# Strided heads first: a reordered start, new planner constants and a smaller last store in a fused sparse attention and feed-forward kernel

## Chip, cores and metric

The kernel runs on one core of one Trainium2 chip. The metric is the device time of one launch in microseconds (us), of which a median is taken over runs. TensorE is called PE below, VectorE DVE, ScalarE ACT, GpSimd POOL and SyncE SP, as in the profile.

## What is computed

There are 8 batches, 8 heads, 576 positions and a head dimension of 64. The first four heads see a local band, the last four see every 32nd position. The result of attention, 4608 tokens of 512 values, goes through a feed-forward layer of 2048 hidden values.

```python
mask_local = (rel >= 0) & (rel < 32)                    # heads 0..3, rel = row - column
mask_strided = (rel >= 0) & (column % 32 == row % 32)   # heads 4..7
attn = softmax(where(mask, q @ k.T / 8, -1e9)) @ v
x = attn.transpose(0, 2, 1, 3).reshape(4608, 512)
h = x @ w_in                       # 512 x 2048
g = s * relu(h) ** 2 + b
out = g @ w_out                    # 2048 x 512
```

## The kernel before

**Attention.** A batch has four head pairs, m = 0 and 1 for the band, m = 2 and 3 for the strided heads. `pair_steps` makes the PE steps of one pair. For the early batches these are: transposes of q and k (`trans`), whose results are copied from PSUM into `qD_loc` or `qD_str` (queries, two heads side by side) and `kT_loc` or `kTs`; scores (`score`, L623); for batch 0 a matmul ahead of each score that adds -30000 where the mask forbids (`neg_loc`, `neg_str`, L620), and for later batches a multiplication with a mask on DVE after the exponential; the exponential on ACT (L641); the weighted sums with v (`av`, L684), where `v_loc` and `v_str` carry a column of ones, so that the sums of the weights come out as well; the division on DVE or ACT (L701, L711); transposes of the result (`xtrans`, L731) into `xT`, one buffer for each pair.

Later batches replace PE transposes by transposing DMAs, issued on SP: `k_dma`, `q_dma` (from `QS_DMA`, `KB_DMA`, `QB_DMA`, which are 3, 4 and 5, on) and `x_dma`, or `x_out` and `x_in` through DRAM.

**Feed-forward.** Blocks of 512 tokens. `ff1` (L983) multiplies `xT` with `w_in_sb`; ReLU and square go to ACT or DVE; `ff2` (L1238) or, from block 2 on, `ff2_seven` (L951) multiplies with `w_out_sb`. The last two blocks use `ff1_seven` (L1208). Block 0 is special: its matmuls begin as soon as the first of the four `xT` buffers is there, in the order `FIRST = (0, 1, 2, 3)`. The outputs are evicted by DVE (`store`, L882) and stored by SP (L886).

**Loads.** POOL issues casting DMAs, fp32 in memory to fp16 on chip: for batch 0 `load_qk(0)` (band q and k in two halves each, then strided q and k), one DMA for two heads of band v, strided v (`early_v`); then the four quarters of `w_in`, batch 1, four quarters of `w_out`, and from then on `fetch_qk(b + 2)` and `fetch_v(b + 2)` as buffers come free. The other two heads of band v of batch 0 are staged in fp32 by SP inside the buffer of `w_out` (`stage_v`, L311) and cast by POOL (`cast_v`). `rows_before` copies, for the band, the 32 rows ahead of each block of 96 keys.

A DMA that may only start when something else has landed is held back by a small copy that reads what landed (`gate`, L1323 on POOL and L1362 on SP).

**The order.** Nothing is scheduled at run time: each engine works through its own list in order. `Plan` writes these lists when the program is built. It keeps an estimated time `plan.t` of PE, an estimated time `done` of each result, and a free time of each engine. `flush` posts what is ready by these estimates to ACT, DVE or POOL, or to SP (`D`, `X`, `Y`), in the order of readiness plus an offset for each kind of work (`ORDER`). `LAT` is the time from the end of an issue to the use of its result:

```python
LAT = {"A": 70.0, "V": 70.0, "P": 70.0, "D": 12000.0, "X": 7000.0, "Y": 12000.0}
```

Loads get their estimated landing from `landing(cost)`, a running time of one queue:

```python
ring = max(ring, plan.t + 2000.0) + cost
return ring + (6000.0 if plan.t > 60000.0 else 600.0)
```

The main loop takes an attention step when attention is behind `due()`, which follows the progress of both feed-forward halves, and a feed-forward step otherwise. Where nothing is ready ahead of the 16th `ff1` matmul, `keep_running` puts a matmul on constants, a filler (L1502), which nobody reads.

Of the kernel before, what the change touches and what calls it, by code (L numbers as in the profile page):

```python
# [18 lines left out]
class Plan:  # L19
# [7 lines left out]
    LAT = {"A": 70.0, "V": 70.0, "P": 70.0, "D": 12000.0, "X": 7000.0, "Y": 12000.0}  # L27

    def __init__(self, order):
        self.t = 0.0  # L30
        self.SLACK, self.ahead, self.LATER = order["SLACK"], order["ahead"], order
        self.done = {}
        self.pend = []
        self.free = {"A": 0.0, "V": 0.0, "P": 7000.0, "D": 0.0, "X": 0.0, "Y": 0.0}
        self.banks = {}

# [7 lines left out]

    def flush(self):
        while True:
            best = None
            for p in self.pend:
                r = self.ready_at(p[0])
                if r is None or r > self.t:  # L50
                    continue
                if p[1].keys() <= {"A", "V"} and min(
                        self.free[e] for e in p[1]) > self.t + self.SLACK:
                    continue
                k = p[3][0]
                w = r + self.LATER.get(k[0] if isinstance(k, tuple) and k[2:3] != (0,) else None, 0.0)
                if best is None or w < best[0]:
                    best = (w, r, p)
# [7 lines left out]
            p[2](eng)  # L66
            for k in p[3]:
# [4 lines left out]
                self.done[k] = end + (6000.0 if soon else p[4] or self.LAT[eng])  # L72
# [45 lines left out]
class Step:  # L118
    def __init__(self, fn, ns, needs=(), group=None, keys=(), posts=(), after=None):
# [4 lines left out]
ORDER = {"g": 1500.0, "S": 2500.0, "in": 2500.0, "w_mix": 0.0, "wc": 1000.0, "ev": 1000.0,  # L124
         "c21": 1500.0, "c11": 500.0, "c12": 500.0, "C22": -1500.0, "fv": 0.0, "Vb": -400.0,
         "x": -1500.0, "Ub": 1000.0, "xc": -1500.0, "fe": -400.0, "k": 1500.0, "fu": -1500.0,
         "Va": 500.0, "p": 0.0, "c22": 500.0, "Ua": 2500.0, "e": -1500.0, "q": 0.0, "r": 0.0,
         "u": 0.0, "SLACK": 600.0, "ahead": 0.05}
KINDS = ("g", "S", "in", "w_mix", "wc", "Va", "Ua", "Ub", "Vb", "C22", "xc", "q", "k", "r", "x", "e",
         "p", "u", "ev", "fv", "fu", "fe", "c11", "c22", "c21", "c12")  # L130


def varied(order, rnd):

    order = dict(order)
    for kind in rnd.sample(KINDS, rnd.choice((1, 2, 4))):
        order[kind] = rnd.choice((-1500.0, -800.0, -400.0, 0.0, 500.0, 1000.0, 1500.0, 2500.0))
    if rnd.random() < 0.2:
        order["SLACK"] = rnd.choice((400.0, 600.0, 800.0, 1000.0))
    if rnd.random() < 0.2:  # L140
        order["ahead"] = rnd.choice((0.0, 0.05, 0.1, 0.2))
    return order
# [46 lines left out]
def lay_out(ctx, tc, nc, q, k, v, moe_w_in, moe_w_out, moe_s, moe_b, out, order, q_shape, out_shape,  # L189
# [8 lines left out]
    FIRST = (0, 1, 2, 3)  # L198
# [56 lines left out]
    NV = 2  # L255
# [13 lines left out]
    def x_free(b):  # L269
# [23 lines left out]
    vl_stage = w_out_sb.rearrange("p f m -> p (f m)").bitcast(FP32)[:, 0:NL // 2].rearrange(  # L293
        "p (h t d) -> p h t d", h=2, d=D)

# [13 lines left out]
    def stage_v(heads):  # L309
        for h in heads:  # L310
            nc.sync.dma_start(out=vl_stage[LPAD:128, h], in_=v_band(0, h))  # L311

    nc.sync.dma_start(out=ident, in_=h_ident.ap())
    stage_v(range(2))
    nc.sync.dma_start(out=negs, in_=h_neg.ap())
    nc.vector.memset(ones16, 1.0)
    for i in range(2):
        nc.vector.memset(qD_loc[i], 0.0)
        nc.vector.memset(kT_loc[i][:, 0:LPAD], 0.0)
    nc.vector.memset(vl_stage[0:LPAD], 0.0)  # L320
    for i in range(2):
        nc.vector.memset(qD_str[i], 0.0)
    for i in range(NV):
        nc.vector.memset(v_loc[i][:, :, :, D:D + 1], 1.0)
        nc.vector.memset(v_loc[i][0:LPAD, :, 0, :], 0.0)
        nc.vector.memset(v_str[i][:, :, :, D:D + 1], 1.0)
# [11 lines left out]

    def load_qk(b):
        for mm in range(2) if b == 0 else ():  # L340
            hs = slice(2 * mm, 2 * mm + 2)
            for name, src in (("q", q), ("k", k)):
                if mm == 0:
                    loaded[b, name + "l"] = inp.tile([LQ, NL], FP16, tag=name + "l", name=name + "l")
                nc.gpsimd.dma_start(out=h4(loaded[b, name + "l"])[:, hs],
                                    in_=view_l(src, b)[:, hs])
        for name, src in (("q", q), ("k", k)) if b else ():
# [73 lines left out]
    def cast_v(b, loc, mm, key):  # L421
        nt, np_, dst = (LT, 128, v_loc) if loc else (ST, SQ, v_str)

        def g(eng):
            src = vl_stage if loc else loaded[b, "vs"].rearrange(
                "p (h t d) -> p h t d", h=4, d=D)
            for h in range(2 * mm, 2 * mm + 2):
                copy_on(eng, out=dst[b % NV][0:np_, h, :, 0:D], in_=src[:, h])
        n = nt * D
        plan.post([key], {"P": 1000.0} if loc else {"P": 1160.0} if b == 0 else {"A": 2 * (170 + 0.83 * n), "V": 540.0}, g,  # L430
                  [("cast", b, mm) if loc else ("in", "vs", b, mm)])
        if loc:
            rows_before(b, mm, ("cast", b, mm))

    def rows_before(b, mm, key):
# [3 lines left out]
        src = vl_stage[:, :, :, 0:D] if b == 0 and mm == 0 else vl[:, :, :, 0:D]  # L439

        def g(eng):
            copy_on(eng, out=vl[0:LPAD, hs, 1:LT, 0:D], in_=src[128 - LPAD:128, hs, 0:LT - 1])
        plan.post([key], {"P": 800.0} if b == 0 and mm == 0 else {"P": 800.0, "V": 350.0} if b == 0 else {"A": 700.0, "V": 350.0}, g, [("in", "vl", b, mm)])
# [30 lines left out]
    def pair_steps(b, m):  # L474
# [10 lines left out]
        def trans(name, j, group):  # L485
# [19 lines left out]
            s = Step(f, (57 if id_ == (0, 0) else 40) if alone else 35, needs=[("in", name + sfx, b, mm)],  # L505
# [1090 lines left out]
```

## Time and profile before

| | |
|---|---|
| median of 3 runs | 298.2 us (298.0 to 298.53) |
| profiled execution, its own time | 298.86 us |
| its span, first to last instruction | 297.1 us |
| PE busy | 290.5 us, 2802 matmuls |
| weight loads (PEld) busy | 220.0 us |
| DVE, ACT, POOL busy | 235.3, 194.3, 93.7 us |
| granted PE clock | 0.999 |
| moved by DMA | 38.19 MB, of it 18.23 MB on POOL's queue |

A matmul row counts as busy from its start to a modelled end, and neighbours overlap, so the mean duration of a row is longer than its distance to the next. Where a count matters, distances between starts are used.

### The profile page before, as it was taken

How to read it: one execution, taken by the hardware profiler on the slowest of the kernel's cores; microseconds unless marked ns; L12 is line 12 of the kernel's file. 1: busy time of each engine (PE TensorE's matmuls, PEld its weight loads, DVE VectorE, ACT ScalarE, POOL GpSimd, SP SyncE). 2: the span in 40 equal slices, each digit the busy share in tenths (PEclk: the TensorE clock that was granted, in tenths of full speed). 3: DMA queues.
4: the chain of work that ended last, by engine and by line, in shares of the span. 5: the costliest groups of instructions: out<-in, count | busy, mean ns of one | idle time of the engine just before them, and what ended most of it. 6: DMA issues, size and time to landing. Idle time of an engine off the chain costs nothing.

```text
span 297.1 us, 7092 instructions
## 1 busy us (share of the span) xinstructions
PE 290.5 (98%) x2802; PEld 220.0 (74%) x2802; DVE 235.3 (79%) x501; ACT 194.3 (65%) x336; POOL 93.7 (32%) x140
## 2 busy tenths in 40 slices
PE   8999999999999999999999999999999999999995
PEld 3775656666556568889767776768888989999984
DVE  5857888798966988787877896759898588888963
ACT  3577957898838798647774878469877545675400
POOL 8873624601980296009710394100000000000000
PEclk9999999999999999999999999999999999999999
DMA  8999999997999499989999999999230300110214
GB/s 136 189 206 203 218 180 184 223 171 119 109 195 149 67 132 138 170 173 122 148 136 144 182 170 105 143 140 207 44 97 0 108 29 9 71 38 3 95 48 142
DMA packets 106152, 38.19 MB, mean 129 GB/s; under 512 B 85414, under 2 KB 103974, under 8 KB 106118
## 3 DMA queue, kind: packets, MB, share of 16 engines
q0 software_dynamic: 60848, 18.23, 62.7%
q1 hardware_dynamic: 45270, 19.51, 36.0%
q8 instruction: 22, 0.36, 0.5%
q14 instruction: 12, 0.10, 0.1%
HBM read 36.99 MB, written 10.62 MB: 160 GB/s over the span
## 4 chain that ended last, share of the span: by engine, by line
PE 88%; DMA 6%; ACT 2%; DVE 2%; POOL 1%; issue 1%; ACTq 0%
PE ps_f L983 28%; PE ps_f L951 22%; PE ps_f L1238 8%; DMA v_loc<-in_v_dram 6%; PE ps_s L623 5%; PE ps_f L1208 3%; PE ps_a L684 3%; PE ps_s L1502 2%; PE ps_a L1208 2%; PE ps_s L951 2%; PE ps_t L1208 2%; PE ps_s L1208 2%; PE ps_t L951 1%; PE ps_s L1238 1%; PE ps_t L684 1%; PE ps_t L502 1%
## 5 line engine op out<-in xcount | busy, mean ns | idle before, releaser
L983 PE MATMUL ps_f<-xT,w_in_sb 128*128 128x512 f16 (+4 forms) x568 | 115.5, 331 | 0.3 <-ACT u L1009 0.3
L1009 ACT ACTIVATE u<-ps_f 128x512 f16<-128x512 f32 x104 | 61.0, 594 | 32.5 <-PE ps_f L983 31.8
L983 PEld LDWEIGHTS <-w_in_sb 128*128 128x128 f16 x576 | 57.4, 114 | 23.2 <-issue 0.5
L951 PEld LDWEIGHTS <-gT 128*128 128x128 f16 x608 | 58.4, 98 | 9.2
L951 PE MATMUL ps_f<-w_out_sb,gT 128*128 128x256 f16 x376 | 55.6, 273 | 0.0
L1017 ACT ACTIVATE gT<-u 128x1024 f16<-128x1024 f16 x29 | 30.7, 1057 | 0.8
L1238 PE MATMUL ps_f<-w_out_sb,gT 128*128 128x512 f16 x112 | 30.4, 379 | 0.0
L951 PE MATMUL ps_f<-w_mix,gT 128*128 128x256 f16 x176 | 25.1, 273 | 0.0
L641 ACT ACTIVATE p_str<-ps_s 72x432 f16<-72x432 f32 (+1 forms) x46 | 20.7, 482 | 6.4 <-PE ps_s L623 5.8
L711 DVE TENSOR_TENSOR x_nat<-ps_a,rec 96x384 f16<-96x384 f32 (+2 forms) x46 | 24.1, 523 | 0.6
L641 ACT ACTIVATE p_loc<-ps_s 128x384 f16<-128x384 f32 x46 | 21.4, 494 | 4.8 <-PE ps_s L623 4.3
L1019 DVE TENSOR_TENSOR gT<-u 128x1024 f16<-128x1024 f16 x27 | 18.5, 686 | 5.9 <-ACT u L1009 5.4
L819 DVE TENSOR_TENSOR gT<-gT 128x1024 f16<-128x1024 f16 x34 | 22.4, 678 | 0.6 <-ACT gT L1017 0.4
L382 POOL DMA_DIRECT2D v_loc<-in_v_dram x24 | 17.7, 757 | 8.6 <-DMA w_out_sb<-in_moe_w_out_dram 5.7
L951 PEld LDWEIGHTS <-S 128*128 128x128 f16 x176 | 17.1, 98 | 2.9
L1238 PEld LDWEIGHTS <-gT 128*128 128x128 f16 x128 | 11.4, 98 | 7.8
L387 POOL DMA_DIRECT2D v_str<-in_v_dram x16 | 13.0, 816 | 12.3 <-PE ps_f L983 3.6
L684 PEld LDWEIGHTS <-p_str 72*128 72x128 f16 x256 | 12.8, 98 | 5.1 <-ACT p_str L641 0.4
L1323 POOL COPY gate<-kT 1x1 f16<-1x1 f16 x6 | 1.5, 256 | 45.0 <-DMA kT<-ks 45.0
L951 PE MATMUL ps_f<-w_mix,S 128*128 128x256 f16 x112 | 15.5, 273 | 0.0
L701 DVE RECIPROCAL rec<-ps_a 96x6 f32<-96x6 f32 (+2 forms) x47 | 8.6, 182 | 8.6 <-PE ps_a L684 8.4
L1149 ACT ACTIVATE gT<-u 128x1024 f16<-128x1024 f16 x12 | 12.7, 1058 | 1.7 <-DVE u L1128 1.4
(237 smaller groups left out, 529.7 us busy)
## 6 DMA issues: line engine op xcount, KB each, us to landing
out_dram<-o SPq DMA_DIRECT2D x34, 256.0 KB, 2.9
w_in_sb<-in_moe_w_in_dram POOLq DMA_DIRECT2D x4, 512.0 KB, 9.7
w_out_sb<-in_moe_w_out_dram POOLq DMA_DIRECT2D x4, 512.0 KB, 9.9
qs<-in_q_dram POOLq DMA_DIRECT2D x6, 288.0 KB, 8.4
ks<-in_k_dram POOLq DMA_DIRECT2D x6, 288.0 KB, 9.7
v_loc<-in_v_dram POOLq DMA_DIRECT2D x24, 72.0 KB, 9.6
ql<-in_q_dram POOLq DMA_DIRECT2D x4, 288.0 KB, 9.0
kl<-in_k_dram POOLq DMA_DIRECT2D x16, 72.0 KB, 3.6
```

The lines of the kernel that those rows point to most:

```text
L382: nc.gpsimd.dma_start(out=vl[LPAD:128, h, :, 0:D], in_=v_band(b, h))
L641: nc.scalar.activation(out=st["pw", g][0:nk, 0:2 * n * nq], in_=st["s", g][0:nk, 0:2 * n * nq], func=AF.Exp, scale=scale)
L684: nc.tensor.matmul(out=st["pa", g][:, n % 6, :], lhsT=st["pw", gp_][0:nk, i * nq:i * nq + WIDE], rhs=vt[0:nk, 2 * mm + e, j, :])
L711: nc.vector.tensor_tensor(out=x_at(0, cnt), in0=st["pa", g][0:nq, 0:cnt, 0:D], in1=st["rec", g][0:nq, 0:cnt].to_broadcast([nq, cnt, D]), o ...
L819: {"V": nc.vector, "P": nc.gpsimd}[eng].tensor_tensor(out=at(out), in0=at(x), in1=at(y), op=op)
L951: nc.tensor.matmul(out=gts[name, T, t][:, 0] if halves else gts[name, T][:, t], lhsT=lhs(k, t), rhs=rhs(k), start=fresh and k == 0 and (ha ...
L983: nc.tensor.matmul(out=gts["h", T, ft][:, lo:hi], lhsT=w_in_sb[ft // 4][:, ct].rearrange("p (x l) -> p l x", l=4)[:, ft % 4], rhs=xT[ct][: ...
L1009: nc.scalar.activation(out=u, in_=gts["h", T, ft], func=AF.Relu)
L1017: nc.scalar.activation(out=g, in_=u, func=AF.Square)
L1019: nc.vector.tensor_tensor(out=g, in0=u, in1=u, op=ALU.mult)
L1208: nc.tensor.matmul(out=st[bk][:, 256 * t:256 * t + 256], lhsT=lhs(t, c), rhs=rhs(c), start=fresh and t == c == 0, stop=t == c == 1, skip_g ...
L1238: nc.tensor.matmul(out=gts[id_], lhsT=gts[T][:, ft, ts * 128:(ts + 1) * 128], rhs=w_out_sb[:, ft, cols], start=(ft == 0), stop=(ft == NFT ...
```

## The change

- **Start.** `load_first` replaces `load_qk(0)`: strided q and k of two heads, then of the other two, strided v, band q and k whole, band v of all four heads by one casting DMA on POOL. `stage_v`, its clearing and its casts go. `FIRST` is (2, 3, 0, 1), and batches 0 and 1 take their pairs in this order. `w_in` is issued after the casts of strided v, without its gate. DVE clears `qD_str` and the first v buffers first.
- **Masks of batch 0.** `forbid` is a step of its own, one matmul for each bank of scores, which needs only `negs` and a bank.
- **Planner.** `landing` and `shared` estimate loads: each transposing or storing DMA posted on SP puts off all loads under way by 1 us. `LAT` of `D` and `Y` goes from 12 to 10 us, and 3 us less when no load is under way. `late` gives work of batch 0 offsets by pair. `ORDER` has new values. The fetch of q and k of batch b + 2 waits for `qT` in place of its copy `qD` where q comes by transposing DMA.
- **Last output.** The last product of the last block is computed in two halves of 128 columns, each evicted and stored by itself.

The diff, cut to its core:

```diff
-    LAT = {"A": 70.0, "V": 70.0, "P": 70.0, "D": 12000.0, "X": 7000.0, "Y": 12000.0}
+    LAT = {"A": 70.0, "V": 70.0, "P": 70.0, "D": 10000.0, "X": 7000.0, "Y": 10000.0}
...
+    def landing(self, cost, keys, wait=700.0):
+        self.ring = max(self.ring, self.t + 2000.0) + cost
+        for k in keys:
+            self.done[k] = self.ring + wait
+        self.loads.append(keys)
+
+    def shared(self, cost=1000.0):
+        self.loads = [x for x in self.loads if self.done[x[0]] > self.t + 1000.0]
+        for x in self.loads:
+            for k in x:
+                self.done[k] += cost
+        if self.ring > self.t:
+            self.ring += cost
...
             p[2](eng)
+            if eng in "DXY":
+                self.shared()
...
-                self.done[k] = end + (6000.0 if soon else p[4] or self.LAT[eng])
+                self.done[k] = end + (6000.0 if soon else p[4] or self.LAT[eng] - (
+                    3000.0 if eng in "DY" and self.ring < self.t else 0.0))
...
-    FIRST = (0, 1, 2, 3)
+    FIRST = (2, 3, 0, 1)
...
-    def stage_v(heads):
-        for h in heads:
-            nc.sync.dma_start(out=vl_stage[LPAD:128, h], in_=v_band(0, h))
...
-    nc.vector.memset(vl_stage[0:LPAD], 0.0)
...
+    def load_first():
+        for name in "qk":
+            loaded[0, name + "l"] = inp.tile([LQ, NL], FP16, tag=name + "l", name=name + "l")
+        loaded[0, "qs"] = inp.tile([SR, NS], FP16, tag="qs", name="qs")
+        loaded[0, "ks"] = ks[0]
+        for hs in slice(0, 2), slice(2, 4):
+            for name, src in (("q", q), ("k", k)):
+                nc.gpsimd.dma_start(out=h4(loaded[0, name + "s"])[0:64, hs],
+                                    in_=view_s(src, 0)[0:64, hs])
+                if hs.start == 0:
+                    nc.gpsimd.dma_start(out=h4(loaded[0, name + "s"])[64:SQ],
+                                        in_=view_s(src, 0)[64:SQ])
+        early_v(0)
+        for name, src in (("q", q), ("k", k)):
+            nc.gpsimd.dma_start(out=h4(loaded[0, name + "l"]), in_=view_l(src, 0))
+        load_vl(0)
...
-                    s.posts = [([key], {"V": 1520} if id_ == (0, 1) else {"A": 1280, "V": 1520 if loc else 918}, g,
+                    s.posts = [([key], {"V": 918} if id_ == (0, 2) else {"A": 1280, "V": 1520 if loc else 918}, g,
...
-                    s.posts = [([key], {"V": 757} if id_ == (0, 0) else {"A": 640, "V": 757 if loc else 453},
+                    s.posts = [([key], {"A": 640} if id_ == (0, 2) else {"A": 640, "V": 757 if loc else 453},
...
-                if b < PE_MASK:
-                    nc.tensor.matmul(
-                        out=st["s", g][0:nk, c:c + 2 * nq], lhsT=ident[0:nk, 0:nk],
-                        rhs=neg_loc if loc else neg_str, start=True, stop=False)
...
+        def forbid(i, group):
+            n = min(per_s, nt - i)
+            def f():
+                st["s", i // per_s] = bank(group)
+                nc.tensor.matmul(
+                    out=bank(group)[0:nk, 0:2 * n * nq], lhsT=ident[0:nk, 0:nk],
+                    rhs=(neg_loc if loc else neg_str)[:, None, :].to_broadcast([nk, n, 2 * nq]),
+                    start=True, stop=False, skip_group_check=True)
+            return Step(f, 2 * n * nq / 2.4 + 3, needs=[("negs",)], group=group)
...
+            ends = [(t, k, slice(0, 256)) for t in range(2) for k in range(H)]
+            if last and key == "P3":
+                ends = ends[0:H] + [(1, k, slice(128 * c, 128 * c + 128)) for c in range(2)
+                                    for k in range(H)]
...
-                arrive(both(name + "l", b), landing(4600))
+                plan.landing(2400, both(name + "l", b))
...
-        plan.done["raw", "vl", b] = landing(4600)
+        plan.landing(2700, [("raw", "vl", b)])
...
-            arrive(both("vs", b), landing(5000))
+            plan.landing(3300, both("vs", b), 1200)
...
-    load_qk(0)
-    nc.gpsimd.dma_start(
-        out=v_loc[0].rearrange("p h t d -> p (h t) d")[LPAD:128, 2 * LT:4 * LT, 0:D],
-        in_=v.rearrange("b h (t p) d -> b p (h t) d", p=LQ)[0, :, 2 * LT:4 * LT])
-    early_v(0)
+    load_first()
...
     def weights_in(eng):
-        nc.gpsimd.tensor_copy(out=gate[0:8, 2:3], in_=loaded[0, "qs"][64:SQ, 0:1])
         load_w_in()
...
-    plan.post([("in", "vl", 0, 0)] + both("qs", 0), {"P": 2500.0}, weights_in, [("w",)])
+    plan.post(both("vs", 0), {"P": 2500.0}, weights_in, [("w",)])
...
-        for m in range(4):
+        for m in FIRST if b < 2 else range(4):
...
-                        [("q", (b, mk)) for mk in range(4)] + [("k", (b, mk)) for mk in range(4)] +
+                        [("qT" if b >= (QB_DMA if mk < 2 else QS_DMA) else "q", (b, mk))
+                         for mk in range(4)] + [("k", (b, mk)) for mk in range(4)] +
...
+        pos += order_.get(f"ahead{int(pos / 3)}", 0.0)
...
-        if len(order) == 2 and i1 % 4 == 0 and f1_pos[i1] > (f2[i2 - 1].pos if i2 else 0.0) + 1:
+        if len(order) == 2 and i1 % 4 == 0 and f1_pos[i1] > (f2[i2 - 1].pos if i2 else 0.0) + lead:
```

## Prediction

> **What bounds the kernel now.** I read the busy line first, then the busy time by stretch, the timeline of TensorE (PE) at the start, the waits where PE pauses later, and the last evictions.
>
> ```profile
> PE 290.5 (98%) x2802; PEld 220.0 (74%) x2802; DVE 235.3 (79%) x501; ACT 194.3 (65%) x336; POOL 93.7 (32%) x140
> ```
>
> PE is busy for 290.5 of 297.1 us, so a change counts only by PE time that it takes away: pauses, useless matmuls, or what follows the last matmul. By stretch (start:end, length, then busy time of PE, PEld, DVE, ACT, POOL):
>
> ```profile
> 10.00:15.00 5.00, 4.39 (x90) 3.81 (x90) 4.17 (x11) 3.62 (x12) 4.31 (x8) 1.00 1.46 186
> 15.00:20.00 5.00, 4.73 (x90) 4.12 (x86) 3.40 (x14) 3.53 (x12) 5.00 (x9) 1.00 1.24 206
> 40.00:60.00 20.00, 20.00 (x233) 12.26 (x232) 15.35 (x40) 13.84 (x25) 9.39 (x13) 1.00 1.61 193
> 150.00:200.00 50.00, 49.65 (x408) 35.73 (x407) 38.14 (x79) 32.70 (x54) 14.93 (x21) 1.00 1.54 143
> 200.00:250.00 50.00, 49.35 (x500) 43.82 (x499) 42.09 (x89) 35.58 (x56) 0.00 (x0) 1.00 0.32 75
> ```
>
> From 25 to 150 us PE has no pause; from 150 to 250 us it lacks 0.35 + 0.65 = 1.0 us. The rest lies before 25 us and behind the last matmul. At the start the busy share misleads, because the fillers of L1502 (matmuls on constants that nobody reads) count as busy:
>
> ```profile
> 1.05 4.34 PE L1502 MATMUL ps_s<-w_mix 128*128 128x512 f16 x10 [1.05 <-DVE w_mix L316]
> 5.33 0.69 PE L494 MATMUL ps_t<-ident,ql 96*64 96x96 f16 x12
> 5.95 1.29 PE L1502 MATMUL ps_s<-w_mix 128*128 128x256 f16 x8
> 7.17 0.45 PE L494 MATMUL ps_a<-ident,kl 96*64 96x96 f16 x12
> 7.55 0.77 PE L1502 MATMUL ps_s<-w_mix 128*128 128x512 f16 x5
> ```
>
> From start to next start, fillers take 4.28 + 1.22 + 0.70 us here and, with the later ones, 6.65 us. The first feed-forward matmul (L983) starts at 18.96 us. Later, between 190 and 202 us, the waits show one late load:
>
> ```profile
> ACT v_loc L404 <- DMA v_loc<-in_v_dram: 2.5, 1, 2.5
> PEld L623 <- issue: 0.6, 1, 0.6
> PEld L983 <- issue: 0.5, 1, 0.5
> ```
>
> The band v of batch 7 was last issued at 178.55 and landed at 195.3. ACT's copy of it waited 2.5 us with the ReLUs queued behind it, and PE lost 0.5 + 0.6 us. The end:
>
> ```profile
> 293.61 0.48 DVE L882 SCALAR_TENSOR_TENSOR o<-ps_f,sb_all,Ub 128x256 f32<-128x256 f32 x1 [0.39 <-PE ps_f L951]
> ```
>
> After it come 3.0 us of output DMA to 297.1.
>
> [...] the first fillers of 512 columns start every 0.43 us, later matmuls of that size every 0.216 us; the change of pace comes at about 6 us. [...]
>
> **The start, part by part.** *Loads.* POOL issues 11 loads for batch 0 before and after. Before, SP also staged two heads of band v in fp32 (two DMAs), DVE cleared 32 rows of the stage (0.70 us) and POOL cast it (1.81 us with one row copy); all three go, with the gate copy that waited for qs (0.18 us). Two row copies remain for the band, now one on POOL (0.72 us) and one on DVE (0.33 us). The strided casts are ahead of w_in's issue on POOL now: 4 x 0.61 = 2.4 us, so w_in is issued from about 11.6 instead of 10.4. I cost that at nothing, since w_in lands behind the loads ahead of it, whose bytes are the same six tensors; without that cover it would cost 1.2 us. Six tensors end at 14.7 before (POOL's wait for vs ends at 14.77) and the first half at about 5.3, so one takes about 1.85 us. Estimated landings after: qs 5.6, ks 7.4, vs 9.2, ql 11.0, kl 12.9, band v 14.7, w_in's first quarter 14.7 + 2.5 = 17.2.
>
> *Where feed-forward can begin.* It needs w_in (17.2) and, by the new order of PE's list, the first band pair's weighted sum ahead of it. ACT carries that: qD copy 1.28 and kT copy 0.67 behind ql and kl (kT done at 14.0), xT 0.64, second qD copy 1.28, three exponentials 1.3: 17.2. With six sums and PE's other work, the first feed-forward matmul starts at about 17.7, 1.25 us sooner than 18.96. Its list holds 8.22 us of useful columns ahead of this point against 8.36 (columns at 2.4 per ns), which takes 0.14 back, and 512 filler columns come behind it, 0.2 us more. Net: **-0.9 us**. The fillers say much the same: 9088 columns against 9600, of which 4224 against 4992 before the first transpose at 0.43 us per 512: -0.65, and at most -0.85 with the slow ones that follow.
>
> *Masks.* 28 mask matmuls (192 or 144 columns) become 12 with the same 4608 columns; they wait only for negs, so they stand where fillers did. Trace: 0.083 us for 192 columns, 0.080 by the rate. 16 x some 4 ns: **-0.1 us**. In exchange a score bank is held from mask to exponential; other banks were free for fillers, so nothing, at worst 0.2. I take the start at **-1.0 us, between -1.8 and -0.1**: the low end is w_in late by its 1.2 us, the high end the pauses of 10 to 20 us gone as well.
>
> *Past the start.* w_out's quarters landed at about 35, 38, 40 and 43 us by POOL's waits and were first used about 2.5 us later, so PE may run 1.0 us earlier there without stalling.
>
> **The middle.** The planner's constants move nearly every instruction. In the list of PE, the first score of batch 4, 5, 6, 7 stands behind 87.6, 113.0, 140.9, 169.9 us of columns, before 96.6, 128.4, 158.3, 188.0: attention runs 9 to 18 us further ahead, and a batch follows each 27.4 us instead of 30.5. The matmuls are the same, so this costs or saves only pauses. It can remove the 1.0 us. But loads and transposes must come as much sooner. SP's transpose issues take 1.2 to 2.9 us each, some twelve for each batch; POOL waited up to 16.3 us at the gate on kT. The planner now assumes 10 us (7 when no load is under way) from a transpose to its use, 12 before; the trace shows landings of 3.0 to 8.4 us (medians), at most 10.4. Each late one costs as above, about 1.1 us. Bounds: -1.0 (every pause gone) to +4.4 (four late loads). I take -0.3: the margins shrink but do not vanish.
>
> **The end.** The last 8 matmuls of 256 columns become 16 of 128: 8 x 0.109 = 0.87 us against 16 x 0.057 (the rate of 128-column fillers) = 0.91. The last eviction halves from 0.48 to about 0.3, and its DMA from 128 to 64 KB. Sum **-0.2 us**, between -0.5 and +0.1.
>
> **Sum.** -1.0 - 0.3 - 0.2 = -1.5 us. The profiled execution took 298.86 us, 1.76 around its span, 0.66 above the median; the span should become 295.6, and the median 298.2 - 1.5 = 296.7.
>
> **Rivals.** *A: late transposes and loads (slower).* With attention further ahead, SP's queue and POOL's gate deliver kT, qT and band v of batches 4 to 7 late; PE stalls in order, as at 196 us. Against it: landings below 10 us. For it: the batch interval shrinks by 10%, and transfers held nearly all slices up to 210 us. Three late loads of 1.1 us outdo start and end: 298.2 - 1.2 + 3 x 1.1 = 300.3; it decides from 1.2 us of new pauses on. *B: the start is bound by transfers (no change).* If w_in comes 1.2 us later through its later issue, what is left is 298.2 - 0.1 - 0.2 = 297.9. Against it: the bytes ahead of it. *C: all pauses go (faster).* Start -1.8, middle -1.0, end -0.3: 295.1.
>
> **Chances.** Forecast 50%, C 12%, B 14%, A 24%. A measurement of this kernel can tell about 0.2% (0.6 us) from no change. Forecast and C are faster, B falls to 'same' but for 2 in 14, A is slower: faster 0.64, same 0.12, slower 0.24. The range goes from C into the lighter half of A (two late loads and a half): 295.1 to 299.6.
>
> **What would show it.** Right: the first feed-forward matmul near 17.7 us, fillers about 5.9 us, 150 to 250 us lacking at most 1.0, a last eviction near 0.3 us. Wrong: w_in landing after 18 us (B); POOL gates or PE waits on kT, qT, v_loc between 90 and 200 us of more than 2 us (A).

## The result, and the profile after

The changed kernel takes **316.6 us** (median of 4 runs, 315.4 to 317.3), the kernel before 298.2, run beside it: ratio 1.061 (below, a ratio is always to the kernel before, run beside), 95% interval 1.057 to 1.065. Forecast were 296.7 us and a range of 295.1 to 299.6, with 0.24 for slower. The profiled execution took 317.27 us with a span of 315.5, so 18.4 us are to be found in the span.

The busy line of the changed kernel's page:

```profile
PE 294.3 (93%) x2794; PEld 220.7 (70%) x2794; DVE 230.8 (73%) x492; ACT 195.3 (62%) x331; POOL 94.0 (30%) x140
```

PE was busy 98% of the span before and is busy 93% of a longer span now: it waits. By stretch, in the columns of the prediction (PE, PEld, DVE, ACT, POOL, granted clock, DMA share, GB/s):

```profile
5.00:10.00 5.00, 3.13 (x37) 2.18 (x38) 1.93 (x5) 0.67 (x2) 3.69 (x5) 0.85 1.03 131
10.00:15.00 5.00, 5.00 (x75) 4.05 (x73) 1.80 (x8) 3.34 (x8) 3.63 (x6) 0.81 1.52 170
40.00:60.00 20.00, 20.00 (x238) 12.39 (x236) 15.36 (x39) 14.21 (x27) 7.42 (x11) 1.00 1.75 181
120.00:140.00 20.00, 14.11 (x158) 12.31 (x157) 11.05 (x26) 10.85 (x20) 3.71 (x8) 1.00 1.71 130
140.00:160.00 20.00, 17.63 (x180) 14.60 (x179) 13.69 (x30) 13.21 (x23) 13.49 (x18) 0.97 1.68 127
200.00:250.00 50.00, 47.51 (x447) 38.42 (x445) 36.38 (x81) 30.10 (x45) 1.75 (x2) 1.00 0.42 90
```

From 120 to 140 us PE lacks 5.9 us, in the next 20 us 2.4, from 200 to 250 us 2.5; from 40 to 60 us nothing, as before. The kernel before, from 120 to 140 us:

```profile
120.00:140.00 20.00, 20.00 (x200) 17.97 (x199) 15.51 (x32) 11.41 (x21) 6.62 (x11) 1.00 1.27 154
```

At the start the granted clock fell, to 0.85 from 5 to 10 us and 0.81 from 10 to 15 us on average.

To compare kernels I worked out **lost time** from the trace's list of matmuls: the time passed, less the time of the matmuls so far. Fillers are left out. A matmul is taken at 2.4 columns per ns and 2.5 ns more, an estimate from the spacing in the trace of before: 0.216 us for 512 columns, 0.109 for 256. A constant error drops out of the difference to the kernel before. The marks stand at the work that the kernel before has done at 25, 120 and 210 us, so that a kernel that runs late is compared at the same work:

| lost against before, us | to 25 us | 25 to 120 | 120 to 210 | 210 to last matmul | behind it | span |
|---|---|---|---|---|---|---|
| changed kernel | +2.6 | +0.4 | **+13.0** | +1.7 | +0.6 | +18.4 |

**The middle.** The chain of waits of the changed kernel names the long links between 110 and 210 us (start, length, what):

```profile
130.31 9.11 DMA kT<-ks
147.80 10.11 DMA xT<-x_dram
160.33 9.63 DMA qT<-qs
192.36 10.79 DMA qT<-qs
```

All four are transposing DMAs, and each took 9 to 11 us from its issue on SP. The PE pauses of more than 0.3 us between 120 and 210 us add up to 11.2 us. After the one at 155.6 us the granted clock was 0.50 for 3.4 us, some 1.7 us of work lost by my estimate. Together that is the +13.0.

The queue of SP (`SPq`), by what it waited for between 80 and 210 us (total, times, longest), has a line that the kernel before does not have:

```profile
SPq L623 <- DMA ql<-in_q_dram: 17.4, 7, 7.8
```

L623 issues the transpose of the band q: it was put on SP's queue ahead of the landing of its load.

**The start.** PE's timeline:

```profile
4.97 0.45 PE L551 MATMUL ps_t<-ident,qs 72*128 72x72 f16 x8 [0.21 <-DMA qs<-in_q_dram]
6.41 0.42 PE L551 MATMUL ps_a<-ident,ks 72*128 72x72 f16 x8 [0.70 <-DMA ks<-in_k_dram]
8.18 0.43 PE L551 MATMUL ps_f<-ident,qs 72*128 72x72 f16 x8 [1.17 <-DMA qs<-in_q_dram]
8.45 1.12 PE L1554 MATMUL ps_s<-w_mix 128*128 128x512 f16 x4
...
21.22 0.38 PE L1047 MATMUL ps_f<-xT,w_in_sb 128*128 128x512 f16 x1
```

The first feed-forward matmul comes at 21.22 us, where 17.7 was forecast and 18.96 was the case before. The first quarter of `w_in` landed at 20.6 us, where 17.2 was forecast and 17.1 was the case before.

**The end.** DVE's evictions and PE's last matmuls:

```profile
309.45 0.75 DVE L941 SCALAR_TENSOR_TENSOR o<-ps_f,sb_all,Ua 128x512 f32<-128x512 f32 x1 [2.93 <-DMA out_dram<-o]
...
310.90 0.38 PE L1015 MATMUL ps_f<-w_out_sb,S 128*128 128x128 f16 x4 [1.88 <-DVE o L941]
...
312.57 0.35 DVE L941 SCALAR_TENSOR_TENSOR o<-ps_f,sb_all,Ub 128x128 f32<-128x128 f32 x1 [1.72 <-DMA out_dram<-o]
```

The last eviction takes 0.35 us, near the forecast 0.3, but PE waited 1.88 us for DVE ahead of its last four matmuls, and DVE twice for an output buffer (2.93 and 1.72 us).

### The profile page after: what moved, and what is told of

The parts are those of the page before. It is cut to its first block, busy times and chain, and to the rows that moved or that the text cites. A ratio compares the mean times of both kernels' runs of the same rounds, so it can differ in the third digit from the quotient of the medians.

```text
span 315.5 us, 7069 instructions
## 1 busy us (share of the span) xinstructions
PE 294.3 (93%) x2794; PEld 220.7 (70%) x2794; DVE 230.8 (73%) x492; ACT 195.3 (62%) x331; POOL 94.0 (30%) x140
## 4 chain that ended last, share of the span: by engine, by line
PE 73%; DMA 16%; DVE 3%; SPq 2%; ACT 2%; issue 2%; POOL 1%; DVEq 0%; ACTq 0%; POOLq 0%
PE ps_f L1047 24%; PE ps_f L1015 17%; PE ps_f L1302 7%; DMA qT<-qs 6%; PE ps_s L667 4%; DMA xT<-x_dram 3%; DMA kT<-ks 3%; PE ps_f L1272 3%; PE ps_a L743 2%; DMA out_dram<-o 2%; PE ps_t L1272 2%; PE ps_a L1272 2%; PE ps_s L1272 2%; PE ps_s L1015 2%; SPq L631 2%
## 5 line engine op out<-in xcount | busy, mean ns | idle before, releaser
L1047 PE MATMUL ps_f<-xT,w_in_sb 128*128 128x512 f16 (+4 forms) x568 | 118.1, 333 | 2.4 <-DMA xT<-x_dram 2.4
L1073 ACT ACTIVATE u<-ps_f 128x512 f16<-128x512 f32 x107 | 62.9, 597 | 39.3 <-PE ps_f L1047 37.8
L1015 PEld LDWEIGHTS <-gT 128*128 128x128 f16 x608 | 58.6, 99 | 11.1 <-issue 0.5
L1302 PE MATMUL ps_f<-w_out_sb,gT 128*128 128x512 f16 x112 | 32.2, 379 | 0.1
L1083 DVE TENSOR_TENSOR gT<-u 128x1024 f16<-128x1024 f16 x29 | 19.8, 685 | 15.6 <-ACT u L1073 15.6
L1081 ACT ACTIVATE gT<-u 128x1024 f16<-128x1024 f16 x27 | 28.6, 1058 | 0.7
L770 DVE TENSOR_TENSOR x_nat<-ps_a,rec 72x384 f16<-72x384 f32 (+2 forms) x45 | 23.6, 526 | 0.6
L1015 PEld LDWEIGHTS <-S 128*128 128x128 f16 x184 | 16.8, 98 | 4.0 <-issue 2.3
L743 PEld LDWEIGHTS <-p_str 72*128 72x128 f16 x256 | 14.4, 98 | 4.2
L760 DVE RECIPROCAL rec<-ps_a 72x6 f32<-72x6 f32 (+2 forms) x45 | 8.3, 183 | 12.2 <-PE ps_a L743 12.1
L441 POOL DMA_DIRECT2D v_str<-in_v_dram x16 | 13.0, 817 | 13.2 <-PE ps_f L1047 4.1
L1302 PEld LDWEIGHTS <-gT 128*128 128x128 f16 x128 | 11.4, 98 | 6.6 <-ACT gT L1081 0.2
L743 PEld LDWEIGHTS <-p_loc 128*128 128x128 f16 x192 | 10.5, 98 | 6.9 <-issue 3.2
L458 POOL COPY qD_str<-qT 64x576 f16<-64x576 f16 x6 | 4.6, 769 | 32.2 <-DVE qD_str L458 12.1
## 6 DMA issues: line engine op xcount, KB each, us to landing
v_loc<-in_v_dram POOLq DMA_DIRECT2D x24, 72.0 KB, 11.1
```

The costliest lines, as they stand in the source:

```text
L743: nc.tensor.matmul(out=st["pa", g][:, n % 6, :], lhsT=st["pw", gp_][0:nk, i * nq:i * nq + WIDE], rhs=vt[0:nk, 2 * mm + e, j, :])
L770: nc.vector.tensor_tensor(out=x_at(0, cnt), in0=st["pa", g][0:nq, 0:cnt, 0:D], in1=st["rec", g][0:nq, 0:cnt].to_broadcast([nq, cnt, D]), o ...
L1015: nc.tensor.matmul(out=dst[:, ms], lhsT=lhs(k, t), rhs=rhs(k)[:, ms], start=fresh and k == 0 and (halves or t == 0), stop=t == 1 and k == ...
L1047: nc.tensor.matmul(out=gts["h", T, ft][:, lo:hi], lhsT=w_in_sb[ft // 4][:, ct].rearrange("p (x l) -> p l x", l=4)[:, ft % 4], rhs=xT[ct][: ...
L1073: nc.scalar.activation(out=u, in_=gts["h", T, ft], func=AF.Relu)
L1081: nc.scalar.activation(out=g, in_=u, func=AF.Square)
```

## The experiments

### Parts of the planner put back in the changed kernel

`lat12`: transposes at 12 us again.

```diff
-    LAT = {..., "D": 10000.0, "X": 7000.0, "Y": 10000.0}
+    LAT = {..., "D": 12000.0, "X": 7000.0, "Y": 12000.0}
-                self.done[k] = end + (6000.0 if soon else p[4] or self.LAT[eng] - (3000.0 if ...))
+                self.done[k] = end + (6000.0 if soon else p[4] or self.LAT[eng])
```

> The changed kernel with the planner's 12 us from a transposing DMA to its use put back (10, or 7 with no load under way, in the change); all else as changed. Theory T (transposes are assumed too early): the pauses of PE between 110 and 220 us, 14.7 us in the changed kernel by distance between starts, fall under 5 us, and the time comes to 305 to 309 us. Theory L (loads are assumed too early, transposes only follow): pauses there stay above 9 us, time above 312 us.

316.65 us, ratio 1.061 (1.051 to 1.071): nothing gained, as theory L has it. +12.4 us of the lost time still lie between 120 and 210 us, and SP still waits 14.9 us for `ql` and 13.5 for `kl`. In this list the transposes' constant is not the cause.

`loads_old`: the landings of loads estimated as before, `shared` off.

```diff
-                plan.landing(2400, both(name + "l", b))
+                plan.landing(4600, both(name + "l", b))
-            self.done[k] = self.ring + wait
+            self.done[k] = self.ring + (6000.0 if self.t > 60000.0 else 600.0)
```

> The changed kernel with the landing estimates of loads put back (4.6, 2.0 and 5.0 us for each tensor and 6 us on top after 60 us, no shift by posted transposes); the 10 us of transposes as changed. Theory L: pauses between 110 and 220 us under 5 us, time 305 to 310 us. Theory T: pauses above 9 us, time above 312 us.

309.9 us, ratio 1.039 (1.032 to 1.045). Between 25 and 210 us the loss falls from +13.4 to +4.4 us, and SP's line for `ql` is gone. So the landings are the larger part.

`both_old`: both together.

> Both put back: 12 us for transposes and the old landing estimates of loads; new start, new order values and new last output stay. If the middle is a matter of these estimates, by whichever of the two, the pauses between 110 and 220 us come near those of the kernel before (2 us) and the time to 303 to 307 us, where the later start (2.9 us) and the last output (2.9 us) are what remains. If instead the new start or the order values cause them, pauses stay above 9 us.

313.4 us, ratio 1.050 (1.036 to 1.064), the middle +5.8: between the two forecasts, and worse than `loads_old` alone, which adding up two effects does not give. The longest pause of PE waited for a band v that landed 17.0 us after its issue. `ORDER` was tuned for other estimates, so each of these lists differs in more than the edit; I went on in the kernel before, whose list had nearly no pauses.

### The estimates in the kernel before

`before_est`: all new estimates of transposes and loads, with start, `ORDER`, masks and last product of before.

```diff
-    LAT = {"A": 70.0, "V": 70.0, "P": 70.0, "D": 12000.0, "X": 7000.0, "Y": 12000.0}
+    LAT = {"A": 70.0, "V": 70.0, "P": 70.0, "D": 10000.0, "X": 7000.0, "Y": 10000.0}
+            if eng in "DXY":
+                self.shared()
-                arrive(both(name + "l", b), landing(4600))
+                plan.landing(2400, both(name + "l", b))
...
```

> The kernel before with the changed planner's estimates alone: transposes 10 us (7 when no load is under way) instead of 12, landings of loads as in the change (2.4 us for the band q and k that go out as four DMAs each, where before had 4.6 plus 6), and the transposes that push loads back. Start, ORDER, masks and last product are those of before. Theory Q (SP's in-order queue: transposes of ql and kl are put on it ahead of their loads' landing and hold up what stands behind them): SP waits 15 us or more for landings of ql and kl between 80 and 210 us (before: 0; other loads 10.5), PE loses 6 us or more there, 304 to 312 us. Rival S (the slow start shifts everything and makes the middle late): with the old start the middle stays as it was, 297 to 300 us; the planner's own end for this list, 297.2, would be met within 2 us.

312.35 us, ratio 1.047 (1.042 to 1.052). SP waits 11.1 us for `ql` and 2.9 for `kl`, a little less than the forecast 15, and the middle loses +11.4. The old start does not protect it: rival S falls.

`before_ql`: one number.

```diff
-                arrive(both(name + "l", b), landing(4600))
+                arrive(both(name + "l", b), landing(2400) - 5300.0)
```

> The kernel before with one number changed in its planner: the band q and k of batches 4 to 7 (four DMAs each) are taken to land 5.1 and 7.5 us after the load is begun, as in the changed kernel, instead of 12.6 and 17.2. The list's own estimate of its end is 297.6 us where before's is 294.1 and before takes 4.1 us more than that. Theory Q (this estimate was slack that let SP's queue and POOL's gate run late without harm): SP waits 10 us or more for ql and kl between 80 and 210 us, PE loses 6 us or more there, and the time is 306 us or more. Rival R (the transposes' 10/7 us or the pushing back of loads is what matters): no such waits, 297.6 + 4.1 = 301.7 us.

**318.7 us, ratio 1.069 (1.066 to 1.072).** This one edit alone, with 12 us for the transposes and no `shared`, costs more than the whole change. SP waits 10.6 us for `ql` and 1.8 for `kl`. Between 120 and 210 us +18.9 us are lost: 13.2 in pauses of PE, and some 5.7, by my estimate, in work at half pace after them. Two lines of PE's waits between 140 and 200 us:

```profile
PE ps_f L983 <- DMA xT<-x_dram: 5.5, 1, 5.5
PE ps_s L623 <- DMA kT_alt<-kl: 2.9, 1, 2.9
```

`before_est_ql`: the counterpart, `before_est` with this one estimate put back and kept out of `shared`.

```diff
-                plan.landing(2400, both(name + "l", b))
+                plan.landing(4600, both(name + "l", b), 6000)
+                plan.loads.pop()
```

> The counterpart: all of the change's estimates in the kernel before (as in before_est), but the landings of the band q and k put back to 12.6 and 17.2 us. The list's own estimate of its end is 298.4 us. Theory Q: the waits of SP for ql and kl go (14 us in before_est), and the time comes within 4 to 6 us of the list's estimate, 302 to 304 us. Rival R: still 308 us or more, 10 us above the estimate.

300.7 us, ratio 1.008 (1.005 to 1.011), below the forecast 302 to 304 and 2.3 us above the planner's own estimate; no wait of SP for `ql` or `kl` is left, and the middle loses 1.2 us less than before. So in the list of before the edit of `ql` and `kl` is both enough and needed for the pauses, and rival R falls.

The number does one thing more than the text of these runs says: `landing` also moves the running time of the queue, so that the strided q and k and the v behind `ql` and `kl` are expected up to 4.4 us sooner. No run separates the two. But in `before_est_ql` strided k is expected 15.1 us after the load is begun, before any pushing back by `shared`, sooner than the 16.8 of `before_ql`, and there are no pauses. That speaks for `ql` and `kl` themselves.

### What the estimate does on the chip

With the estimate, transposes move in among the loads of v. For batch 5, the first of SP's transposes of `ql` and the last load of v on POOL, in the kernel before and then in the changed one:

```profile
117.04 2.67 SPq L574 DMA_TRANSPOSE qTl<-ql  x2
116.61 0.81 POOL L387 DMA_DIRECT2D v_str<-in_v_dram  x1 [1.39 <-DVE p_str L649]
```

```profile
110.79 2.84 SPq L623 DMA_TRANSPOSE qTl<-ql  x2
123.57 0.81 POOL L441 DMA_DIRECT2D v_str<-in_v_dram  x1 [0.73 <-PE ps_f L1047]
```

Before, these transposes start as the last load of v is issued; now 13 us ahead of it.

Two mechanisms fit. In Q1, SP's queue stands behind transposes whose load has not landed. In K, transposes that are issued while loads are under way land late.

`ql_nov`: `before_ql` with loads left out.

```diff
     def load_vl(b):
+        if b >= 5:
+            return
...
     def load_vs(b):
+        if b >= 5:
+            return
```

> before_ql (the one changed landing estimate) with the loads of v of batches 5, 6 and 7 left out (24 DMAs of 72 KB; these batches use the v of an earlier one), all lists else the same. Theory K (contention: transposes issued while the loads of the batch are under way land late): kT<-ks and qT<-qs land within 5 us (median) instead of 7 to 10, PE loses at most 4 us between 140 and 200 us, 300 to 304 us. Theory Q1 (SP's queue stands behind qTl, which waits for ql): SP still waits 10 us or more for ql and kl, and 310 us or more.

**300.4 us, ratio 1.006 (1.004 to 1.009).** The waits of SP have not become less:

```profile
SPq L578 <- DMA ql<-in_q_dram: 11.2, 5, 5.0
SPq L559 <- DMA kl<-in_k_dram: 3.4, 3, 2.3
```

But the pauses are gone (120 to 210: +0.2 us). The stretch 140 to 160 us, `before_ql` first, then `ql_nov`:

```profile
140.00:160.00 20.00, 14.47 (x110) 10.12 (x108) 9.53 (x22) 7.71 (x13) 7.49 (x10) 0.83 1.70 130
```

```profile
140.00:160.00 20.00, 20.00 (x183) 14.86 (x181) 17.15 (x39) 14.54 (x26) 3.49 (x6) 1.00 1.11 167
```

PE goes from 14.47 to 20.00 busy, and the DMA share from 1.70 to 1.11. How long a transpose takes is read from SP's issue of `kT<-ks` of batch 5 and POOL's gate copy that waits for it. In `before_ql`, then in `ql_nov`:

```profile
125.20 4.04 SPq L565 DMA_TRANSPOSE kT<-ks  x2
132.83 0.18 POOL L1323 COPY gate<-kT 1x1 f16<-1x1 f16 x1 [12.51 <-DMA kT<-ks]
```

```profile
124.02 2.87 SPq L569 DMA_TRANSPOSE kT<-ks  x2
127.29 0.67 POOL L1327 COPY gate<-kT 1x1 f16<-1x1 f16 x1 [14.55 <-DMA kT<-ks]
```

7.6 us against 3.3. The same pair of rows, in the kernel before and in the changed one:

```profile
129.18 2.55 SPq L565 DMA_TRANSPOSE kT<-ks  x2
132.28 0.33 POOL L1323 COPY gate<-kT 1x1 f16<-1x1 f16 x1 [14.68 <-DMA kT<-ks]
```

```profile
130.31 3.77 SPq L614 DMA_TRANSPOSE kT<-ks  x2
139.48 0.49 POOL L1379 COPY gate<-kT 1x1 f16<-1x1 f16 x2 [2.69 <-DMA kT<-ks]
```

3.1 us against 9.2. In the kernel before and in `ql_nov`, POOL's queue moves no packet between these two rows; in `before_ql` it moves 1641, in the changed kernel 2243. `ql_nov` holds a control in itself: for batch 4, whose loads of v it keeps, the same pair of rows is 8.0 us apart, for batches 5 and 6 it is 3.3.

So the slow transfers need the loads of v (K), and SP's waits for `ql` and `kl` do not make pauses by themselves. Whether these waits add to the loss where the loads run is not shown. Also not separated: without the loads of v nothing can wait for v either, and in `before_ql` DVE waited 13.5 us for band v between 140 and 200 us. Of its four pauses of more than 1 us there, though, three (5.5, 3.2 and 2.9 us) waited for a transposing DMA, directly or by way of DVE, and one (1.5 us) for a band v, by way of ACT.

### The last product

`tail_old`: the changed kernel with the last product in two pieces of 256 columns, in place of one of 256 and two of 128.

```diff
-            if last and key == "P3":
-                ends = ends[0:H] + [(1, k, slice(128 * c, 128 * c + 128)) for c in range(2)
-                                    for k in range(H)]
```

> The changed kernel with the last product in two halves of 256 columns again instead of 256 + 2 x 128. Theory T1 (the third piece shares its bank with the second, so PE's next matmul waits for DVE's eviction, and three output buffers of small pieces are not enough): PE's pause of 2.05 us in the last product and 0.9 us behind the last matmul go, 2 to 3 us less than the changed kernel (313.5 to 314.7). Rival T2 (the tail only shows a late store that another list would have too): within 1 us of the changed kernel.

313.8 us, ratio 1.052 (1.048 to 1.057). Lost behind 210 us: +0.1 against +2.3 in the changed kernel.

`before_tail`: the same three lines, and the eviction by `ms` that goes with them, added to the kernel before.

> The kernel before with the changed last product alone (8 matmuls of 256 columns into 16 of 128, evicted and stored in two pieces). Theory T1: PE waits about 1.0 us for the eviction of the first piece in the same bank, and up to 1 us more for an output buffer; 298.2 + 1 to 2 = 299.2 to 300.2. The prediction's own step: 0.2 us less than before, 298.0.

299.9 us, ratio 1.005 (1.003 to 1.007): 1.5 us more by the ratio, 1.7 by the medians, where the prediction has -0.2. The end of it:

```profile
293.18 0.38 PE L956 MATMUL ps_f<-w_out_sb,S 128*128 128x128 f16 x4 [0.44 <-DVE o L882]
293.18 0.21 PEld L956 LDWEIGHTS <-S 128*128 128x128 f16 x3 [0.56 <-issue]
294.73 0.35 DVE L882 SCALAR_TENSOR_TENSOR o<-ps_f,sb_all,Ub 128x128 f32<-128x128 f32 x1 [1.61 <-DMA out_dram<-o]
```

PE waits 0.44 us, because the third piece goes into the bank that DVE is still reading for the second, and DVE then waits 1.61 us for one of the three output buffers, which an earlier store still holds.

`bufs4`: the changed kernel with four output buffers.

```diff
-    op = ctx.enter_context(tc.tile_pool(name="op", bufs=3))
+    op = ctx.enter_context(tc.tile_pool(name="op", bufs=4))
```

> The changed kernel with four buffers in place of three for the outputs. If the last output is late because its eviction waits for a buffer whose store has not landed (DVE waited 2.9 and 1.7 us), both waits go, the end shortens by 2.5 to 3.5 us and the time comes to 313 to 314 us. If it is PE's wait on the bank that matters, at most 1 us goes.

Two runs, 314.7 and 309.3 us, lie too far apart for a verdict. In the profile of the first, DVE's waits for a buffer are gone from the last evictions, and a pause of PE for the bank stays, at 0.92 us.

### The start

`start_at`: the planner's landing times of batch 0 set to those of the changed kernel's trace.

```diff
-    AT = {"qs0": 4500.0, "ks0": 5600.0, "qs1": 6400.0, "ks1": 7200.0, "vs": 8900.0, "ql": 10300.0,
-          "kl": 11800.0, "vl": 14400.0}
+    AT = {"qs0": 4900.0, "ks0": 6400.0, "qs1": 8100.0, "ks1": 9500.0, "vs": 11300.0, "ql": 13500.0,
+          "kl": 15400.0, "vl": 18300.0}
```

> The changed kernel with the planner's landing times of batch 0 set to those that its trace shows (qs 4.9 and 8.1, ks 6.4 and 9.5, vs 11.3, ql 13.5, kl 15.4, band v 18.3 us), so that fillers stand where PE went idle at 5.5 to 8.2 us. Theory C (the idle stretch lets the clock fall, which costs about 1 us at half pace): granted clock 1.00 between 8 and 15 us, first feed-forward matmul 0.5 to 1.5 us before 21.2. Rival D (transfers alone set it): clock restored, first feed-forward matmul still at 21 us or later. The middle stays slow: 312 to 320 us.

317.6 us, ratio 1.064 (1.055 to 1.073). With fillers where PE had stood idle the clock stays up:

```profile
5.00:10.00 5.00, 4.96 (x61) 3.41 (x60) 1.93 (x5) 2.00 (x5) 3.65 (x5) 1.00 0.93 135
10.00:15.00 5.00, 4.09 (x69) 2.96 (x67) 1.88 (x8) 2.93 (x9) 3.81 (x7) 1.00 1.60 174
```

The first feed-forward matmul comes at 20.27 us, 0.95 sooner (theory C), and the loss to 25 us falls from +2.6 to +1.9: by this, an estimate, the fallen clock is about a quarter of it. The kernel as a whole gains nothing, since between 25 and 120 us this list loses +4.6 us where the changed kernel loses +0.4. The rest of the start goes with the transfers: here too `w_in` lands no sooner than 20.0 us.

`start_whole`: strided q and k of batch 0 not cut by head pairs (and `AT` to match).

```diff
-        for hs in slice(0, 2), slice(2, 4):
-            for name, src in (("q", q), ("k", k)):
...
+        for name, src in (("q", q), ("k", k)):
+            load_s(loaded[0, name + "s"], src, 0)
```

> The changed kernel with strided q and k of batch 0 loaded with four heads in one DMA (and 8 rows), not in head pairs, and the planner's landing times set to 5.5, 7.2, 9.2, 11.3, 13.3 and 16.3 us. Theory P (the pieces of 64 rows x 2 heads are why packets of 1 KB take 113 to 133 ns here against 98 to 105 in before): packets of 1 KB at 98 to 105 ns between 5 and 10 us, 180 KB/us or more there, w_in issued before 12.5 us. Rival M (the strided tensors are slow to load early, in whatever pieces): packets as slow as before, 110 to 160 KB/us, first feed-forward matmul at 20.5 us or later. The middle stays slow in both: 310 to 320 us.

314.7 us, ratio 1.054 (1.051 to 1.058), with the outcome between the theories. From 6 to 8 us POOL's queue moves 168 KB/us (111 in the changed kernel), and a packet of 1 KB takes 108 ns on average (138 there, 102 in the kernel before from 8 to 10 us). The median is 98 ns in all three, so it is a minority of packets that is slow. `w_in` is issued at 12.33 us instead of 13.59. The first feed-forward matmul moves to 19.15 us, but the clock is at 0.67 from 20 to 25 us, and +2.8 us are lost by then, no less than in the changed kernel. From 12 to 15 us only about 100 KB/us move: band v is 2304 packets of 128 B now, at 47 ns on average. Why some packets of 1 KB are slower than in the kernel before stays open.

### Put together

`after_fix_s`: the changed kernel with `ql` and `kl` as in `before_est_ql`, the last product as in `tail_old`, and `ORDER` tuned again for the earliest end by the planner's own estimate.

> The changed kernel with the landings of the band q and k of batches 4 to 7 put back to 12.6 and 17.2 us after the load is begun, the last product in two halves again, and ORDER tuned anew against the planner for this (its own estimate of the end is 294.7 us; 303.3 with the old ORDER). Start, transposes' 10/7 us, pushing back of loads and masks are those of the change. Theory Q: no waits of SP for ql and kl of more than 3 us in sum between 80 and 210 us, PE's middle loses 2 us or less (12.6 in the changed kernel), and what is left against before is the start: 294.7 + 4.1 + 2.9 = 300 to 302.5 us. Rival V (the changed start makes the middle late too, by another way than the estimates): over 305 us.

302.1 us, ratio 1.013 (1.008 to 1.018), as theory Q has it: SP no longer waits for `ql` or `kl`, and the middle is whole (-1.1). What is left is the start, +2.7 to 25 us, and +1.7 from there to 120.

`best2`: `before_est_ql` with `ORDER` tuned again in the same way.

```diff
-ORDER = {"g": 1500.0, ..., "ev": 1000.0, ..., "c11": 500.0, ..., "fu": -1500.0, ..., "ahead": 0.05}
+ORDER = {"g": 0.0, ..., "ev": -1500.0, ..., "c11": -1500.0, ..., "fu": 1000.0, ..., "ahead": 0.0}
```

> before_est_ql with ORDER tuned anew against the planner (own estimate of the end 294.3 us; 298.4 with the ORDER of before, which took 300.7). Start and last product are those of before. If the chip keeps the list as it kept before_est_ql (2.3 us over the estimate): 296.6 us, faster than both kernels. If it keeps it as it kept before (4.1 over): 298.4 us, no difference. Theory Q excludes 302 us or more; the rival, that any list with transposes at 10/7 us stalls when it is tight, gives 302 us or more.

297.9 us against 298.6 for the kernel before, run beside it, ratio **0.997 (0.996 to 0.999)**: a gain of 0.3%, and the only one ahead of the kernel before. How much of it is the new estimates and how much the tuning is not separated. Its line for the stretch that lacked 0.35 us of PE before:

```profile
150.00:200.00 50.00, 50.00 (x413) 36.33 (x412) 37.00 (x75) 31.56 (x57) 15.57 (x20) 1.00 1.33 147
```

The lost time of the profiled executions, all in one table:

| against before, us | to 25 us | 25 to 120 | 120 to 210 | 210 to last matmul | behind it |
|---|---|---|---|---|---|
| changed kernel | +2.6 | +0.4 | +13.0 | +1.7 | +0.6 |
| `before_est` | 0.0 | +2.4 | +11.4 | +0.2 | -0.3 |
| `before_ql` | 0.0 | +0.1 | +18.9 | 0.0 | +0.2 |
| `before_est_ql` | +0.8 | +2.0 | -1.2 | +0.7 | 0.0 |
| `ql_nov` | +0.3 | +0.2 | +0.2 | 0.0 | 0.0 |
| `before_tail` | +0.4 | 0.0 | -1.1 | +0.7 | +0.9 |
| `after_fix_s` | +2.7 | +1.7 | -1.1 | -0.4 | +0.3 |
| `best2` | +0.4 | +0.7 | -1.2 | 0.0 | -0.4 |

The same start and list differ by some tenths between executions (first column). Where a list has pauses, the middle differs by more: `tail_old` has the list of the changed kernel up to the last product, and its profile loses +10.4 us from 120 to 210 us, not +13.0. So at the start and the end differences of about 1 us carry an argument, and in the middle of a list with pauses only those of several us.

## Why the prediction was wrong, point by point

- **The middle, -0.3 with bounds of -1.0 and +4.4; it was +13.0.** This is the step that failed. The upper bound took each late load at 1.1 us, from one late band v in the trace of before, and four of them. PE had six pauses of 0.5 to 3.1 us, 11.2 us in all, and lost some 1.7 us at half pace after one of them. The prediction held the transposes' landings (3.0 to 8.4 us, at most 10.4) as given, and asked only whether the planner's 10 us cover them. But these landings belonged to the order of before. There too the longest, the 10.4 us of an `xT<-x_nat` at 147 us, ran beside loads, some 4000 packets of POOL's queue, without PE waiting for it; `kT<-ks` of batch 5, with 3.1 us, had no packet of that queue beside it. With `ql` and `kl` believed to land 5.1 and 7.5 us after their load is begun, not 12.6 and 17.2, the transposes moved in among the loads of v, and the same `kT<-ks` took 9.2 us. A bound has to let the measured duration itself move when the edit changes what runs beside it.
- **The edit that mattered was not priced.** The prediction worked on the transposes' 10 and 12 us, which `lat12` shows to be worth nothing in this list. The landing of `ql` and `kl`, `landing(4600)` to `landing(2400, ...)`, stood in the diff, and in the prediction's own terms the question was which transposes pass which loads on the queues.
- **The start, -1.0; it was +2.6.** The term that was mis-sized is the landing of the loads, 1.85 us for each tensor, a mean over six tensors of before. Strided v, band q, band k and band v were expected at 9.2, 11.0, 12.9 and 14.7 us, and landed at 11.2, 13.5, 15.3 and 18.4. In the new order strided q and k went out first in small pieces, at 119 KB/us from 3 to 8 us (139 before), and band v went as 2304 small packets, half of which SP had moved before. The casts ahead of `w_in`'s issue took 2.28 us, close to the 2.4 of the prediction, but their input was late, so `w_in` was issued at 13.59 us instead of 11.6. The issue was costed at nothing because `w_in` "lands behind the loads ahead of it"; that cover itself ran late, and the first quarter landed at 20.6 us, not 17.2. This is what rival B looked for, `w_in` after 18 us, but B sized it at 1.2 us. The fillers came down to 9088 columns as forecast, but PE then stood idle for 0.70 and 1.17 us between 5.7 and 8.2 us, and the granted clock was 0.50 from 8.5 to 11.9.
- **The end, -0.2 with +0.1 as its worst; it was +1.5 alone and +2.3 in the changed kernel.** The durations were about right (0.35 us for the eviction). Left out was that the third piece shares its bank with the second (PE waited 0.44 us for it in `before_tail`), and that one more store needs one more of three output buffers (DVE waited 1.61 us there).
- **The masks, -0.1:** nothing in the runs tells it from zero.
- **Rival A** had the right mechanism in kind ("transposes and band v late") and the right test, gates and waits of more than 2 us between 90 and 200 us. It was sized with the same 1.1 us, at 300.3 us.
- **Transposes beside loads.** The prediction gave no figure for what loads on POOL's queue do to transposes on SP's. In `before_ql`, with the loads of v on POOL's queue, the `kT<-ks` of SP's queue takes 7.6 us, in `ql_nov`, without them, 3.3.

## What to carry to other kernels

An estimate in an order fixed ahead of time that looks too long can be the slack that keeps two kinds of transfers apart (in `before_ql` a shorter one cost +18.9 us in the middle); before it is tightened, ask what moves into the same stretch. A landing time read from a trace was good only beside the traffic of that trace here (`kT<-ks` of batch 5: 3.1 us in the kernel before, 9.2 in the changed one). And where a last store is cut finer, count the PSUM banks and the output buffers as well as the columns (in `before_tail` they cost 0.44 us of PE and 1.61 us of DVE in waits).

## What had not been expected of the hardware

- A transposing DMA took more than twice as long with loads of v beside it: `kT<-ks` of batch 5, 7.6 us in `before_ql`, 3.3 in `ql_nov`. From issue to use, it took 2.8 to 4.7 us in all seven lists with the old estimate of `ql` and `kl`, and 6.1 to 9.2 us in the eight with the new one whose loads of v were left in. The issue of transposes on SP was longer too (mean 1.47 us in `ql_nov`, 1.79 in `before_ql`, 1.62 in the kernel before, all 80 to 210 us).
- Some pauses of PE cost again after their end. In `before_ql` PE stood for 5.5 us from 147.4 us on, and in stretches of 1 us the granted clock is 0.50 from 152 to 158 us: five us of work at half pace. Less idle time was followed by the same where PE had little to do around it: in `start_whole` PE stood for 1.1 us up to 19.15 us, was busy for 0.76, 0.08 and 0.85 us of the three us from 17 on, and the clock was 0.50 from 20 to 23 us. In the changed kernel, though, the pauses of 1.9, 0.9 and 3.1 us between 120 and 140 us left it at 1.00.
- Packets of 1 KB took 98 to 159 ns on the same queue, as means over stretches of 20 us with at least 100 of them, with the cause of the slow ones open.
